# Windowed attention and a gated MLP in one kernel: the order of the MLP's products, of the weights' splits, and the places of late weight fetches

## The chip, the cores and the metric

The kernel runs on one core of one Trainium2 chip. The metric is device time in microseconds (us) of one execution. The core has a matrix engine (PE; its weight loads are shown as PEld), a vector engine (DVE), an activation engine (ACT), GpSimd (POOL) and a sync engine (SP) that issues most DMAs. The engines run side by side and wait for one another by semaphores; each takes its own instructions in order.

## What is computed

```
k_all, v_all = concat([k_g, k_l]), concat([v_g, v_l])          # 8 batches, 8 heads, 32 + 512 positions, 64 wide
out_g = softmax(q_g @ k_all.T / 8) @ v_all                      # 32 global queries see everything
s_l   = concat([q_l @ k_g.T / 8, where(|i - j| <= 32, q_l @ k_l.T / 8, -1e9)])
out_l = softmax(s_l) @ v_all                                    # local queries: a band and the globals
x = concat([out_g, out_l]) as 4352 rows of 512
h = x @ w_in                                                    # 512 x 2048
return (h * sigmoid(h)) @ w_out                                 # 2048 x 512
```

The inputs are float32, except w_in and w_out, which are float64.

## The kernel before, in words

The 4352 rows make 34 tiles of 128 rows, and the tiles make 12 token blocks n of SIZES = 3, ..., 3, 2, 2 tiles ("pieces"). Attention for a block is done ahead of that block's MLP. It comes as a stream of small steps with due times (`stream`); `advance` issues those that have come due, and `fill` does so in portions between the MLP's matmuls. For each of 128 steps k (a tile and a pair of heads) there are scores `s` on PE, a softmax on DVE and ACT (`probs`, `st`), a transposition and the product `o` with the values. From step 12 on the transposition goes by DMA: POOL copies `probs` into `halves`, SP stores them to DRAM (`away`, L379), and SP loads them back transposed into `pt` (L383). POOL adds the global part to `pt` (L401). `xh` and `xl` are the result in two parts, as below.

float32 products are made from pairs: every operand is a rounded upper part ("hi") and the rest ("lo"), and hi·hi + hi·lo + lo·hi stand for the product. So each product is three matmuls. The weights come as 16 slices f of 128 hidden units. A slice has two halves: w_in's 128x512 (half 0) and w_out's 128x512 (half 1). Each goes through three stages, all within block 0:
- `fetch_weights` (L193, SP): the raw float64 words come as a DMA into `raw_w`, 512 KB a half.
- `join_weights` (L209 on ACT, L211 and L212 on DVE): two 32-bit words become one float32.
- `split_weights` (L221 on ACT: `w_hi`; L222 on DVE: `w_lo`).

The tiles `ws0` to `ws15` hold the joined slice f at ws(f+1), later w_lo of slice f at ws(f). The tiles `wh0` to `wh15` hold first raw halves, later w_hi. Second halves of slices 8 to 15 have no such place: they come in two DMAs of 256 KB into pairs of the attention's tiles `qk` (odd slices) or `klo` (even).

The MLP goes through blocks n and in each through slices f. `first_layer(n, f)` makes twelve matmuls into one accumulator `h`; then tanh (`t`, L587 ACT and L588 DVE), `gh` (L590 ACT) and `gl` (L591 DVE). `second_layer(n, f)` comes one slice later, after the next `first_layer`: three matmuls for each piece into accumulators `out0` to `out2`, which add up over the 16 slices. At a block's end ACT copies them out (L612) and they are stored (L615).

PE's instructions stand in the order of the program text. The other engines' are put in an order by a scheduler when the program is built, except that those marked `hold` keep their mutual order. SP's DMAs stand in one queue.

Of the kernel before, what the change touches and what calls it, by code (L numbers as in the profile page):

```python
# [12 lines left out]
I32 = mybir.dt.int32  # L13
# [8 lines left out]
P = 128  # L22
# [5 lines left out]
SKV = SG + SL  # L28
DM, DFF = H * D, 2048
NCC, NF = DM // P, DFF // P  # L30
QW, KW, VW = 2 * P, 2 * W, 4 * D
# [7 lines left out]
SIZES = (3,) * 10 + (2, 2)  # L39
BUFS = dict(qk=2, raw=2, p=2, halves=1, pt=4)  # L40
# [7 lines left out]
SINGLE = 12  # L48
SCRATCH = 8
FETCH, LOOK = 5, 3  # L50
FIRSTW = {4: 2, 5: 2, 6: 1, 7: 1, 8: 1, 9: 1, 10: 1, 11: 1}
JOINS, SPLITS = (9.0, 9.6, 10.2, 10.8, 11.4, 12.0), (12.1, 12.7)

# [15 lines left out]
def attention_moe_kernel(ctx: ExitStack, tc: tile.TileContext, qk0_in, qk_in, v_in, gqk, wts, out):  # L69
    nc = tc.nc  # L70

    const = ctx.enter_context(tc.tile_pool(name="const", bufs=1))
    raws = ctx.enter_context(tc.tile_pool(name="raws", bufs=BUFS["raw"]))
    work = ctx.enter_context(tc.tile_pool(name="work", bufs=1))
# [33 lines left out]
    def scratch(i, dtype, name):  # L108
        return const.tile([P, 2 * DM], dtype, tag=f"wh{i}", name=name)
# [13 lines left out]
    for kind in range(3):  # L123
# [4 lines left out]
                                     fill=NEG, base=0, channel_multiplier=-1))  # L128
        hold(nc.gpsimd.affine_select(out=band, in_=band, pattern=[[-1, W - SG]], compare_op=ALU.is_ge,
                                     fill=NEG, base=2 * HALO, channel_multiplier=1))  # L130
# [49 lines left out]
    w_32, w_hi, w_lo, w_raw, w_next = [], [], [], {}, [0]  # L180

    def fetch_weights(f, half):
        i = 2 * f + half
        if half and f >= SCRATCH:
            tag, n = ("qk", QW + KW) if f % 2 else ("klo", SKV)
            homes_ = [work.tile([P, n], I32, tag=tag, bufs=BUFS["qk"], name=f"raw_w{i}_{q}")[:, :DM] for q in range(2)]
        else:
            taken.add(f + SCRATCH * half)
            homes_ = [scratch(f + SCRATCH * half, I32, f"raw_w{i}")]
        n = DM // len(homes_)  # L190
        w_raw[i] = [(raw, q * n, n) for q, raw in enumerate(homes_)]
        for raw, c0, n in w_raw[i]:
            hold(nc.sync.dma_start(out=raw, in_=wts[f, :, DM * half + c0 : DM * half + c0 + n].bitcast(I32)))  # L193

    def join_weights():
        i = w_next[0]
        w_next[0] += 1
        f = i // 2
        if f + 1 == NF:
            w_32.append(work.tile([P, SKV], F32, tag="klo", bufs=BUFS["qk"], name=f"w{i}")[:, :DM])  # L200
        elif i % 2 == 0:
            w = const.tile([P, 2 * DM], F32, tag=f"ws{f + 1}", name=f"w{f}")
            w_32.extend((w[:, :DM], w[:, DM:]))
        for raw, c0, n in w_raw[i]:
            join_words(w_32[i][:, c0 : c0 + n], raw)
# [9 lines left out]
    def split_weights(f):  # L215
        w_hi.append(const.tile([P, 2 * DM], F32R, tag=f"wh{f}", name=f"w_hi{f}"))
        w_lo.append(const.tile([P, 2 * DM], F32R, tag=f"ws{f}", name=f"w_lo{f}"))
        for c0 in range(0, 2 * DM, DM):
            sl = slice(c0, c0 + DM)
            hi, lo, w = w_hi[f][:, sl], w_lo[f][:, sl], w_32[2 * f + c0 // DM]  # L220
            hold(nc.scalar.copy(out=hi, in_=w))  # L221
            hold(nc.vector.tensor_tensor(out=lo, in0=w, in1=hi.bitcast(F32), op=ALU.subtract))  # L222
# [257 lines left out]
    def put(when, fn, *a):  # L480
        stream.append((when, fn, a))

    AHEAD = NPR
    for k, (t, b, c, pr) in enumerate(steps):
        a = (k, b, c, pr)
        j = k % NST
# [21 lines left out]
        if j == 0 and b:  # L508
            for hh in range(2):
                put(at + (TURN if b > 1 else TURN1)[hh], g_turn, b, hh)  # L510
        for i in range(FIRSTW.get(k, 0)):
            put(at + 0.01, fetch_weights, *divmod(sum(FIRSTW.get(j, 0) for j in range(k)) + i, 2))
        put(at + due["load"], st_load, *a)
# [10 lines left out]
        if k < SINGLE or pr == NPR - 1:  # L524
            n = 1 if k < SINGLE else NPR
# [17 lines left out]
    def advance(to):  # L543
        nonlocal done
        while done < len(stream) and stream[done][0] <= to:
            _, fn, a = stream[done]
            done += 1
            fn(*a)
# [7 lines left out]
    outs, now = {}, [0, 0]  # L556

    def fill(part):

        now[1] += part  # L560
        n = now[0]
        total = NF * SIZES[n] + (NF - 1) * SIZES[n] + (SIZES[n - 1] if n else 0)
        if n + 1 < len(SIZES):
            advance(ends[n] + (ends[n + 1] - ends[n]) * min(1.0, now[1] / total / FULL))

    def out_rows(t):
        kind, b, c = order[t]
        if kind == "l":
            return [(0, P, b * SKV + SG + c * P)]
        return [(SG * i, SG, (4 * b + i) * SKV) for i in range(4)]  # L570

    def first_layer(n, f):
        nt = SIZES[n] * P
        xh, xl = xblk[n]
        h = ps_h.tile([P, 512], F32, tag="h", name=f"h{n}_{f}")
        i = 0
        for c in range(NCC):
            wh = w_hi[f][:, c * P : (c + 1) * P]
            wl = w_lo[f][:, c * P : (c + 1) * P]
            for wt, x in ((wh, xh), (wh, xl), (wl, xh)):  # L580
                nc.tensor.matmul(h[:, :nt], wt, x[:, c, :nt], start=(i == 0), stop=(i == 3 * NCC - 1))  # L581
                i += 1
        t = two.tile([P, 3 * P], F32, tag="t", bufs=1, name=f"t{n}_{f}")
        gh = two.tile([P, 3 * P], F32R, tag="gh", name=f"gh{n}_{f}")
        gl = two.tile([P, 3 * P], F32R, tag="gl", name=f"gl{n}_{f}")

        nc.scalar.activation(t[:, :nt], h[:, :nt], AF.Tanh, scale=0.5)  # L587
        nc.vector.scalar_tensor_tensor(out=t[:, :nt], in0=t[:, :nt], scalar=1.0, in1=h[:, :nt], op0=ALU.add,  # L588
                                       op1=ALU.mult)
        nc.scalar.copy(out=gh[:, :nt], in_=t[:, :nt])  # L590
        nc.vector.tensor_tensor(out=gl[:, :nt], in0=t[:, :nt], in1=gh[:, :nt].bitcast(F32), op=ALU.subtract)  # L591
        return gh, gl

    def second_layer(n, f, gh, gl):
        if f == 0:
            outs[n] = [ps_out.tile([P, DM], F32, tag=f"out{i}", name=f"out{n}_{i}") for i in range(SIZES[n])]
        wh, wl = w_hi[f][:, DM:], w_lo[f][:, DM:]

        last = n + 1 == len(SIZES) and f == NF - 1
        for i in (reversed(range(SIZES[n])) if last else range(SIZES[n])):  # L600
            o = outs[n][i]
            sl = slice(i * P, (i + 1) * P)
            nc.tensor.matmul(o, gh[:, sl], wh, start=(f == 0), stop=False)  # L603
            nc.tensor.matmul(o, gh[:, sl], wl, start=False, stop=False)  # L604
            nc.tensor.matmul(o, gl[:, sl], wh, start=False, stop=(f == NF - 1))  # L605
            fill(1)
        if f == NF - 1:
            done_ = work.tile([P, 3 * DM], F32, tag=f"xh{n % 2}", name=f"o{n}")
            for i in (reversed(range(SIZES[n])) if last else range(SIZES[n])):
                o = outs[n][i]  # L610
                sb = done_[:, DM * i : DM * (i + 1)]
                nc.scalar.activation(sb, o, AF.Copy, scale=0.5)  # L612
                for p0, np_, r in out_rows(sum(SIZES[:n]) + i):
                    queue = nc.scalar if 0 < n < len(SIZES) - 1 else nc.sync
                    queue.dma_start(out=out[r : r + np_, :], in_=sb[p0 : p0 + np_, :])  # L615

    advance(ends[0])
# [2 lines left out]
    for n in range(len(SIZES)):  # L620
        for f in range(NF):
            if n == 0:
                while w_next[0] < 2 * min(NF, f + LOOK):
                    join_weights()
                for g, half in ((f + FETCH, 0), (f + FETCH - (f + FETCH > SCRATCH), 1)):
                    if g < NF and 2 * g + half not in w_raw:
                        fetch_weights(g, half)
            elif f == 0:
                advance(ends[n])
                now[:] = n, 0  # L630
            while len(w_hi) < NF and len(w_hi) <= NF * n + f + 1:
                split_weights(len(w_hi))
            g = first_layer(n, f)
            fill(SIZES[n])
            if pend is not None:
                second_layer(*pend)
            pend = (n, f, *g)
    second_layer(*pend)


# [67 lines left out]
```

## Time and profile before

| | |
|---|---|
| three runs | 986.2, 988.7 and 989.6 us; median 988.7 |
| profiled execution | 991.2 us, of it a span of 989.4 us from first to last instruction |
| busy, share of the span | PE 97%, PEld 86%, DVE 64%, ACT 58%, POOL 20% |
| granted PE clock | 0.993 of full speed over the span |
| matmuls | 5790, each with its own weight load |
| DMA | 157.3 MB, mean 159 GB/s |
| the three first-layer terms (L581) | 254.4, 254.0 and 252.8 us busy |
| the three second-layer terms (L603 to L605) | 220.9, 214.6 and 215.5 us busy |

Block 0's MLP begins at 48 us and ends at about 154 us. "Idle" and "waited" are time in which an engine's next instruction could not start, and the arrow names what ended it. Matmuls are pipelined, so that a matmul's own duration is longer than the distance from its start to the next one's; the distance is what it costs.

### The profile page before, as it was taken

What the parts mean: (1) busy time and instruction counts of PE and PEld (TensorE: products, weight loads), DVE (VectorE), ACT (ScalarE), POOL (GpSimd) and SP (SyncE); (2) the same over time, 40 slices, a digit from 0 to 9 for tenths busy, and PEclk for the clock granted to TensorE, in tenths of its full rate; (3) what the DMA queues carried; (4) which work ended last, traced back from release to release, by engine and by line L of the source; (5) the groups of instructions that cost most, each with busy time, mean ns of one, the idle gap of its engine ahead of it and who ended that gap; (6) DMA issues with size and microseconds to landing.
All of it is one profiled execution on the core that took longest, in us unless ns stands there. A gap on an engine that the chain in (4) does not pass through costs nothing.

```text
span 989.4 us, 17458 instructions
## 1 busy us (share of the span) xinstructions
PE 961.3 (97%) x5790; PEld 852.9 (86%) x5790; DVE 631.6 (64%) x1910; ACT 577.9 (58%) x1483; POOL 200.6 (20%) x413
## 2 busy tenths in 40 slices
PE   8989889999999999999999999999999999999997
PEld 6668778999898989998899999988989899889896
DVE  4888886766767667655577667766677565453322
ACT  7977756666556656644566666666566665343332
POOL 2112222122222212111222122212122221120000
PEclk9999899999999999999999999999999999999999
DMA  8699967566664666534656586565665564433000
GB/s 274 231 280 267 237 168 198 159 167 179 180 165 124 196 178 166 162 95 132 169 159 154 150 209 172 144 192 145 174 180 161 151 162 139 129 83 82 1 22 23
DMA packets 190026, 157.33 MB, mean 159 GB/s; under 512 B 128752, under 2 KB 148720, under 8 KB 189936
## 3 DMA queue, kind: packets, MB, share of 16 engines
q1 hardware_dynamic: 185712, 148.61, 55.1%
q10 hardware_dynamic: 4224, 7.60, 2.2%
q8 instruction: 46, 0.75, 0.3%
q14 instruction: 44, 0.36, 0.1%
HBM read 86.44 MB, written 39.32 MB: 127 GB/s over the span
## 4 chain that ended last, share of the span: by engine, by line
PE 79%; DVE 7%; DMA 6%; ACT 4%; issue 1%; SPq 1%; POOL 1%; DVEq 0%; ACTq 0%; POOLq 0%
PE h L581 33%; PE out L603 11%; PE out L605 11%; PE out L604 11%; PE o L425 6%; DMA raw<-in_qk_dram 3%; PE s L350 2%; PE s L351 2%; DMA raw_g<-in_gqk_dram 2%; DVE w L212 1%; DMA away<-halves 1%; DVE w_lo L222 1%; PE s L348 1%; ACT probs L359 1%; PE gt L296 1%
## 5 line engine op out<-in xcount | busy, mean ns | idle before, releaser
L581 PE MATMUL h<-xh,w_lo 128*128 128x384 f32 (+1 forms) x768 | 254.4, 331 | 8.8 <-DVE w_lo L222 8.8
L374 POOL COPY halves<-probs 128x512 uint16<-128x512 uint16 x232 | 153.0, 685 | 514.9 <-ACT probs L363 171.8
L581 PE MATMUL h<-xh,w_hi 128*128 128x384 f32 (+1 forms) x768 | 254.0, 331 | 0.4 <-ACT w_hi L221 0.4
L581 PE MATMUL h<-xl,w_hi 128*128 128x384 f32 (+1 forms) x768 | 252.8, 329 | 0.0
L603 PE MATMUL out<-w_hi,gh 128*128 128x512 f32 x544 | 220.9, 406 | 2.5 <-ACT gh L590 2.3
L605 PE MATMUL out<-w_hi,gl 128*128 128x512 f32 x544 | 215.5, 396 | 2.0 <-DVE gl L591 1.9
L604 PE MATMUL out<-w_lo,gh 128*128 128x512 f32 x544 | 214.6, 394 | 0.0
L587 ACT ACTIVATE t<-h 128x384 f32<-128x384 f32 (+1 forms) x192 | 90.4, 471 | 165.5 <-PE h L581 152.7
L588 DVE SCALAR_TENSOR_TENSOR t<-t,h 128x384 f32<-128x384 f32 (+1 forms) x192 | 101.7, 530 | 113.0 <-ACT t L587 112.4
L581 PEld LDWEIGHTS h<-xh,w_lo 128*128 128x128 f32 x768 | 145.6, 190 | 10.9 <-DVE w_lo L222 10.9
L359 ACT ACTIVATE probs<-probs,st 128x224 f32<-128x224 f32 x244 | 115.8, 476 | 65.0 <-DVE st L355 64.1
L581 PEld LDWEIGHTS h<-xh,w_hi 128*128 128x128 f32 x768 | 145.6, 190 | 8.0 <-ACT w_hi L221 0.9
L581 PEld LDWEIGHTS h<-xl,w_hi 128*128 128x128 f32 x768 | 145.5, 190 | 6.6 <-DVE xl L433 0.2
L591 DVE TENSOR_TENSOR gl<-t,gh 128x384 fp32r<-128x384 f32 (+1 forms) x192 | 109.4, 570 | 43.5 <-ACT gh L590 39.1
L355 DVE CUSTOM_DVE_ANT_0 probs<-s,mask 128x224 f32<-128x224 f32 x244 | 86.2, 388 | 78.9 <-PE s L351 66.7
L590 ACT CAST gh<-t 128x384 fp32r<-128x384 f32 (+1 forms) x192 | 94.4, 492 | 59.5 <-DVE t L588 59.2
L605 PEld LDWEIGHTS out<-w_hi,gl 128*128 128x128 f32 x544 | 102.5, 188 | 30.1 <-DVE gl L591 7.2
L603 PEld LDWEIGHTS out<-w_hi,gh 128*128 128x128 f32 x544 | 103.1, 190 | 22.0 <-ACT gh L590 6.1
L604 PEld LDWEIGHTS out<-w_lo,gh 128*128 128x128 f32 x544 | 103.2, 190 | 12.9
L332 ACT CAST qk<-raw 128x704 fp32r<-128x704 f32 x100 | 77.7, 777 | 25.8 <-DMA raw<-in_qk_dram 21.3
L363 ACT ACTIVATE probs<-probs,st 128x224 f32<-128x224 f32 x122 | 58.7, 481 | 43.4 <-DVE st L362 41.4
L333 DVE TENSOR_TENSOR klo<-raw,qk 128x448 fp32r<-128x448 f32 x100 | 64.5, 645 | 28.4 <-ACT qk L332 26.1
(91 smaller groups left out, 1075.8 us busy)
## 6 DMA issues: line engine op xcount, KB each, us to landing
raw<-in_qk_dram SPq DMA_DIRECT2D x100, 352.0 KB, 3.4
away<-halves SPq DMA_DIRECT2D x116, 256.0 KB, 2.8
vraw<-in_v_dram SPq DMA_DIRECT2D x30, 512.0 KB, 4.7
raw_w<-in_wts_dram SPq DMA_DIRECT2D x24, 512.0 KB, 6.6
raw_g<-in_gqk_dram SPq DMA_DIRECT2D x32, 304.0 KB, 4.2
out_dram<-o ACTq DMA_DIRECT2D x28, 256.0 KB, 3.3
raw<-in_qk_dram SPq DMA_DIRECT2D x28, 240.0 KB, 4.3
raw_w<-in_wts_dram SPq DMA_DIRECT2D x16, 256.0 KB, 3.7
```

What stands on the lines that cost most here:

```text
L332: nc.scalar.copy(out=qk, in_=raw)
L355: nc.vector.tensor_tensor_reduce(out=p[:, u, :W], in0=ss[u], in1=mask_of[c], scale=-SCALE, scalar=3.0e38, op0=ALU.add, op1=ALU.min, accum_ ...
L359: nc.scalar.activation(p[:, u, :W], p[:, u, :W], AF.Exp, bias=st[:, u : u + 1], scale=-1.0, accum_out=st[:, 2 + u : 3 + u])
L374: nc.gpsimd.tensor_copy(out=halves[:, :, u], in_=p[:, 2 * P * u : 2 * P * (u + 1)].bitcast(U16).rearrange("p (j h) -> p h j", h=2))
L581: nc.tensor.matmul(h[:, :nt], wt, x[:, c, :nt], start=(i == 0), stop=(i == 3 * NCC - 1))
L587: nc.scalar.activation(t[:, :nt], h[:, :nt], AF.Tanh, scale=0.5)
L588: nc.vector.scalar_tensor_tensor(out=t[:, :nt], in0=t[:, :nt], scalar=1.0, in1=h[:, :nt], op0=ALU.add, op1=ALU.mult)
L590: nc.scalar.copy(out=gh[:, :nt], in_=t[:, :nt])
L591: nc.vector.tensor_tensor(out=gl[:, :nt], in0=t[:, :nt], in1=gh[:, :nt].bitcast(F32), op=ALU.subtract)
L603: nc.tensor.matmul(o, gh[:, sl], wh, start=(f == 0), stop=False)
L604: nc.tensor.matmul(o, gh[:, sl], wl, start=False, stop=False)
L605: nc.tensor.matmul(o, gl[:, sl], wh, start=False, stop=(f == NF - 1))
```

## The change

First, the products are ordered by term. `first_layer` made the three terms for each of the four 128-row chunks c in turn. It now makes hi·hi for all chunks, then hi·lo, then lo·hi. `second_layer` made the three terms for each piece in turn. It now makes gh·w_hi for all pieces, then gh·w_lo, then gl·w_hi, except in a block's last slice, which keeps the order by piece.

Second, slice f + 1 is split at the head of slice f's round in block 0, ahead of the joins and the fetches of that round, and no longer behind them.

Third, the second halves of slices 8, 9, 10, 12 and 13 come in one DMA of 512 KB into `ws15`, `ws14`, `ws13`, `ws14` and `ws15`, the places of later lower weights; those of slices 11 and 14 into `klo` and that of 15 into `qk`, in two pieces as before.

Fourth, ACT issues the very last output DMA, and SP the other four of the last block.

```diff
+PLACES = ("ws15", "ws14", "ws13", "klo", "ws14", "ws15", "klo", "qk")
...
         if half and f >= SCRATCH:
-            tag, n = ("qk", QW + KW) if f % 2 else ("klo", SKV)
-            homes_ = [work.tile([P, n], I32, tag=tag, bufs=BUFS["qk"], name=f"raw_w{i}_{q}")[:, :DM] for q in range(2)]
+            tag = PLACES[f - SCRATCH]
+            if tag in ("qk", "klo"):
+                n = QW + KW if tag == "qk" else SKV
+                homes_ = [work.tile([P, n], I32, tag=tag, bufs=BUFS["qk"], name=f"raw_w{i}_{q}")[:, :DM] for q in range(2)]
+            else:
+                homes_ = [const.tile([P, 2 * DM], I32, tag=tag, name=f"raw_w{i}")]
...
-        for c in range(NCC):
-            wh = w_hi[f][:, c * P : (c + 1) * P]
-            wl = w_lo[f][:, c * P : (c + 1) * P]
-            for wt, x in ((wh, xh), (wh, xl), (wl, xh)):
-                nc.tensor.matmul(h[:, :nt], wt, x[:, c, :nt], start=(i == 0), stop=(i == 3 * NCC - 1))
+        for wt, x in ((w_hi[f], xh), (w_hi[f], xl), (w_lo[f], xh)):
+            for c in range(NCC):
+                nc.tensor.matmul(h[:, :nt], wt[:, c * P : (c + 1) * P], x[:, c, :nt], start=(i == 0),
+                                 stop=(i == 3 * NCC - 1))
                 i += 1
...
-        for i in (reversed(range(SIZES[n])) if last else range(SIZES[n])):
-            o = outs[n][i]
-            sl = slice(i * P, (i + 1) * P)
-            nc.tensor.matmul(o, gh[:, sl], wh, start=(f == 0), stop=False)
-            nc.tensor.matmul(o, gh[:, sl], wl, start=False, stop=False)
-            nc.tensor.matmul(o, gl[:, sl], wh, start=False, stop=(f == NF - 1))
-            fill(1)
+        terms = ((gh, wh), (gh, wl), (gl, wh))
+        if f < NF - 1:
+            order_ = [(i, j) for j in range(3) for i in range(SIZES[n])]
+        else:
+            order_ = [(i, j) for i in (reversed(range(SIZES[n])) if last else range(SIZES[n])) for j in range(3)]
+        for done_, (i, j) in enumerate(order_, 1):
+            g, w = terms[j]
+            nc.tensor.matmul(outs[n][i], g[:, i * P : (i + 1) * P], w, start=(f == 0 and j == 0),
+                             stop=(f == NF - 1 and j == 2))
+            if done_ % 3 == 0:
+                fill(1)
...
-                    queue = nc.scalar if 0 < n < len(SIZES) - 1 else nc.sync
+                    queue = nc.sync if n == 0 or last and i else nc.scalar
...
             if n == 0:
+                split_weights(f + 1) if 0 < f < NF - 1 else None
                 while w_next[0] < 2 * min(NF, f + LOOK):
                     join_weights()
...
-            while len(w_hi) < NF and len(w_hi) <= NF * n + f + 1:
-                split_weights(len(w_hi))
```

The names in the following rows carry the block and the slice (h0_4 is block 0, slice 4), and a number of the buffer behind. Lines of the changed kernel are 3 to 8 higher than before.

On PE, at block 0's slice 4, before: the end of the first layer of slice 4, the scores of step 16, and the second layer of slice 3.

```order
L581 MATMUL h0_4_979<-xh_0_244,w_hi4_912 128x384
L581 MATMUL h0_4_979<-xl_0_245,w_hi4_912 128x384
L581 MATMUL h0_4_979<-xh_0_244,w_lo4_913 128x384
L348 MATMUL s16_1002<-raw16_873 128x224 x2
L603 MATMUL out0_0_804<-w_hi3_843,gh0_3_932 128x512
L604 MATMUL out0_0_804<-w_lo3_844,gh0_3_932 128x512
L605 MATMUL out0_0_804<-w_hi3_843,gl0_3_933 128x512
L603 MATMUL out0_1_805<-w_hi3_843,gh0_3_932 128x512
L604 MATMUL out0_1_805<-w_lo3_844,gh0_3_932 128x512
L605 MATMUL out0_1_805<-w_hi3_843,gl0_3_933 128x512
```

And now, the whole first layer of slice 4 and what follows:

```order
L584 MATMUL h0_4_977<-xh_0_244,w_hi4_899 128x384 x4
L584 MATMUL h0_4_977<-xl_0_245,w_hi4_899 128x384 x4
L584 MATMUL h0_4_977<-xh_0_244,w_lo4_900 128x384 x4
L353 MATMUL s16_1000<-raw16_873 128x224 x2
L611 MATMUL out0_0_804<-w_hi3_832,gh0_3_930 128x512
L611 MATMUL out0_1_805<-w_hi3_832,gh0_3_930 128x512
L611 MATMUL out0_2_806<-w_hi3_832,gh0_3_930 128x512
L611 MATMUL out0_0_804<-w_lo3_833,gh0_3_930 128x512
L611 MATMUL out0_1_805<-w_lo3_833,gh0_3_930 128x512
L611 MATMUL out0_2_806<-w_lo3_833,gh0_3_930 128x512
L611 MATMUL out0_0_804<-w_hi3_832,gl0_3_931 128x512
```

The first matmul that needs w_lo is now the ninth of twelve, and the first that needs gl the seventh of nine; an accumulator is written in turn with the two others.

On the DVE, at the same place before: the joins of slice 5 (raw_w10, raw_w11 into w5), then the lower weights of slice 4.

```order
L281 TENSOR_SCALAR pg1_128<-pg1_128,gst1_1_890 128x544
L211 TENSOR_SCALAR raw_w10_725<-raw_w10_725 128x512
L212 SCALAR_TENSOR_TENSOR w5_899<-w5_899,raw_w10_725 128x512
L211 TENSOR_SCALAR raw_w11_727<-raw_w11_727 128x512
L212 SCALAR_TENSOR_TENSOR w5_899<-w5_899,raw_w11_727 128x512
L222 TENSOR_TENSOR w_lo4_913<-w4_832,w_hi4_912 128x512 x2
L361 TENSOR_SCALAR st15_943<-st15_943 128x2
L591 TENSOR_TENSOR gl0_3_933<-t0_3_931,gh0_3_932 128x384
```

And now:

```order
L286 TENSOR_SCALAR pg1_128<-pg1_128,gst1_1_890 128x544
L227 TENSOR_TENSOR w_lo4_900<-w4_838,w_hi4_899 128x512 x2
L216 TENSOR_SCALAR raw_w10_725<-raw_w10_725 128x512
L217 SCALAR_TENSOR_TENSOR w5_905<-w5_905,raw_w10_725 128x512
L216 TENSOR_SCALAR raw_w11_727<-raw_w11_727 128x512
L366 TENSOR_SCALAR st15_941<-st15_941 128x2
L592 SCALAR_TENSOR_TENSOR t0_4_990<-t0_4_990,h0_4_977 128x384
```

The split stands ahead of the joins; the second half of the join comes some rows later, behind slice 4's tanh product and the next softmax.

On SP, around the second halves of slices 8 and 9 (raw_w17 and raw_w19), before:

```order
L193 DMA raw_w17_0_908<-in_wts_dram 128x512
L193 DMA raw_w17_1_909<-in_wts_dram 128x512
L383 DMA_TRANSPOSE pt2_131<-away14_897 128x4x256
L310 DMA raw17_956<-in_qk0_dram 128x480
L193 DMA raw_w18_971<-in_wts_dram 128x1024
L379 DMA away15_1014<-halves15_999 128x1024
L310 DMA raw18_1024<-in_qk0_dram 128x480
L193 DMA raw_w20_1036<-in_wts_dram 128x1024
L193 DMA raw_w19_0_1038<-in_wts_dram 128x512
L193 DMA raw_w19_1_1039<-in_wts_dram 128x512
L383 DMA_TRANSPOSE pt3_132<-away15_1014 128x4x256
```

And now:

```order
L198 DMA raw_w17_914<-in_wts_dram 128x1024
L388 DMA_TRANSPOSE pt2_131<-away14_897 128x4x256
L315 DMA raw17_954<-in_qk0_dram 128x480
L198 DMA raw_w18_975<-in_wts_dram 128x1024
L384 DMA away15_1012<-halves15_997 128x1024
L315 DMA raw18_1022<-in_qk0_dram 128x480
L198 DMA raw_w20_1040<-in_wts_dram 128x1024
L198 DMA raw_w19_1042<-in_wts_dram 128x1024
L388 DMA_TRANSPOSE pt3_132<-away15_1012 128x4x256
```

The order of the queue is the same; a pair of fetches has become one.

## The prediction

> **What bounds the kernel now.** I read the stretches of the run first, then who waits for whom in each, then single instructions. In the windows the columns after the bounds are the length, then PE, PEld, DVE, ACT and POOL busy, the granted clock, the DMA engines' share and GB/s. The first row is token block 0 from its third weight slice up to its last (slices 2 to 14); the second lies within it; the third is everything after block 0.
>
> ```profile
> 56.90:145.00 88.10, 77.06 (x396) 65.93 (x396) 76.65 (x213) 60.40 (x157) 19.29 (x30) 0.94 0.89 240
> 75.00:100.00 25.00, 23.95 (x144) 21.13 (x144) 22.43 (x64) 18.07 (x48) 6.55 (x10) 1.00 0.93 268
> 152.30:989.40 837.10, 825.32 (x5002) 742.17 (x5000) 512.00 (x1523) 466.99 (x1178) 167.15 (x331) 1.00 0.53 144
> ```
>
> After block 0, PE is busy 825.3 of 837.1 us and DVE 61%: TensorE bounds, and only its own waits can be won. In block 0 PE and DVE are both at 87% (77.1 and 76.7 of 88.1 us), at a clock of 0.94. Who waits there:
>
> ```profile
> PEld h L581 <- DVE w_lo L222: 10.9, 7, 2.9
> PE h L581 <- DVE w_lo L222: 8.8, 5, 2.6
> DVE w L212 <- ACT w L209: 2.6, 6, 0.5
> PE o L425 <- POOL pt L401: 1.0, 1, 1.0
> ```
>
> Nearly all of PE's waiting in block 0 is for the lower weights w_lo that the DVE makes (us in total, times, longest). One such wait, PE and then DVE:
>
> ```profile
> 68.82 0.34 PE L581 MATMUL h<-xh,w_hi 128*128 128x384 f32 x1
> 68.99 0.34 PE L581 MATMUL h<-xl,w_hi 128*128 128x384 f32 x1
> 71.95 0.69 PE L581 MATMUL h<-xh,w_lo 128*128 128x384 f32 x1 [2.62 <-DVE w_lo L222]
> 72.44 0.52 PE L581 MATMUL h<-xh,w_hi 128*128 128x384 f32 x1
> 72.76 0.52 PE L581 MATMUL h<-xl,w_hi 128*128 128x384 f32 x1
> 68.94 0.42 DVE L211 TENSOR_SCALAR raw_w<-raw_w 128x512 uint32<-128x512 uint32 x1
> 69.47 0.69 DVE L212 SCALAR_TENSOR_TENSOR w<-w,raw_w 128x512 uint32<-128x512 uint32 x1
> 70.08 0.42 DVE L211 TENSOR_SCALAR raw_w<-raw_w 128x512 uint32<-128x512 uint32 x1
> 70.61 0.69 DVE L212 SCALAR_TENSOR_TENSOR w<-w,raw_w 128x512 uint32<-128x512 uint32 x1
> 71.21 1.28 DVE L222 TENSOR_TENSOR w_lo<-w,w_hi 128x512 fp32r<-128x512 f32 x2
> ```
>
> The third matmul of slice 4 needs w_lo. The DVE joins the halves of a later slice from 68.94 to 71.21 (2.27 us) before it splits this one. PE stands still until 71.95, and then runs at half pace: starts 0.32 us apart (72.44 to 72.76) where 0.17 is usual (68.82 to 68.99). The same follows a second such wait, of 2.14 us at 106.3; its second-layer matmuls were 0.42 us apart (first two rows), where full pace is 0.22 to 0.23 (last four):
>
> ```profile
> 110.13 0.63 PE L604 MATMUL out<-w_lo,gh 128*128 128x512 f32 x1
> 110.55 0.63 PE L605 MATMUL out<-w_hi,gl 128*128 128x512 f32 x1
> 649.96 0.39 PE L605 MATMUL out<-w_hi,gl 128*128 128x512 f32 x1
> 650.18 0.39 PE L603 MATMUL out<-w_hi,gh 128*128 128x512 f32 x1
> 650.41 0.39 PE L604 MATMUL out<-w_lo,gh 128*128 128x512 f32 x1
> 650.64 0.39 PE L605 MATMUL out<-w_hi,gl 128*128 128x512 f32 x1
> ```
>
> Eighteen first-layer matmuls at about 0.15 us too much and six of the second layer at 0.2 make 3.9 us lost to the lower clock. The Trainium skill (TensorE: Matmul & The Clock Gate, "Why this matters for your kernels") names idle gaps above some 3 us as what drops the clock. The trace shows drops around waits of 2.6 and 2.1 us, so the measurement decides; by that rule the 3.9 us would not hang on these waits, PE's floor below would stay at 77.1, and the floor rival would end at 973.6 instead of 971.2.
>
> **The first layer's order and the earlier split.** All twelve matmuls stay, and so do their weight loads. w_lo is wanted after eight matmuls instead of two: 6 x 0.17 = 1.0 us later. The split stands ahead of the next join, so w_lo comes up to 2.27 us sooner. The 3.3 us together exceed the longest wait (2.9), so taken singly every wait goes: about 11 us, plus 3.9 us of clock. But the joins do not vanish; they move behind the split, and what follows them on the DVE (tanh products, softmax) is late by what w_lo gained. So block 0's floor is a sum of work:
> - PE: 77.06 - 3.9 = 73.2 us.
> - DVE: 76.65 us, less what the larger places save. Five second halves (slices 8, 9, 10, 12 and 13) are now joined whole, not in two pieces (groups of 48 to 152 us):
>
> ```profile
> L212 DVE SCALAR_TENSOR_TENSOR w<-w,raw_w 128x512 uint32<-128x512 uint32 x18 | 13.5, 747 | 3.5 <-ACT w L209 2.6
> L211 DVE TENSOR_SCALAR raw_w<-raw_w 128x512 uint32<-128x512 uint32 x18 | 7.6, 421 | 0.0
> L212 DVE SCALAR_TENSOR_TENSOR w<-w,raw_w 128x256 uint32<-128x256 uint32 x16 | 7.1, 446 | 0.8
> L211 DVE TENSOR_SCALAR raw_w<-raw_w 128x256 uint32<-128x256 uint32 x16 | 5.4, 340 | 0.0
> ```
>
> Two pieces take 2 x (446 + 340) = 1572 ns, one 747 + 421 = 1168: 0.40 us each, 2.0 us for five. So the DVE floor is 74.65 us, and the DVE becomes the slower of the two. How near it gets: from 75 to 100 us, with no long PE wait, it was busy 22.43 of 25 us, 90%. The waits of its L212 for ACT (2.6 of 88.1 us, 3%) should go: the DVE now has the split (1.28 us) to do before its part of a join, while ACT, a step ahead in the same order, does its own. At 93% the stretch takes 74.65/0.93 = 80.3 us: 7.8 us gained. Ends: 90% gives 82.9 (5.2 gained), 96% gives 77.8 (10.3).
>
> **The places.** In the old places a fetch waits until the join two slices earlier is done, and everything behind it on SP stands too:
>
> ```profile
> 83.72 6.04 SPq L193 DMA_DIRECT2D raw_w<-in_wts_dram  x3
> SPq L193 <- DVE raw_w L211: 14.3, 4, 4.9
> ```
>
> Behind this one stand a transpose, an away store and attention loads. The five new fetches find their place unused or joined at least an iteration before, and SP issues five DMAs fewer of the same bytes. PE waited only 1.0 us for attention there, so I cost this at nothing by itself. It is the cover for the faster block: with the same transfers the DMA share of 0.89 rises to 0.89 x 88.1/80.3 = 0.98, and transposed probabilities or raw loads are what is late next.
>
> **The second layer's order.** gl is wanted after six matmuls, not two: 4 x 0.23 = 0.92 us later (not in a block's last slice, which keeps its order). Waits after block 0, and one of them:
>
> ```profile
> PEld out L605 <- DVE gl L591: 6.5, 12, 1.3
> PE out L605 <- DVE gl L591: 1.9, 4, 0.8
> PEld out L603 <- ACT gh L590: 5.6, 13, 1.5
> 653.25 0.50 PE L603 MATMUL out<-w_hi,gh 128*128 128x512 f32 x1
> 653.60 0.39 PE L604 MATMUL out<-w_lo,gh 128*128 128x512 f32 x1
> 654.29 0.50 PE L605 MATMUL out<-w_hi,gl 128*128 128x512 f32 x1 [0.31 <-DVE gl L591]
> 654.63 0.40 PE L603 MATMUL out<-w_hi,gh 128*128 128x512 f32 x1
> ```
>
> Here gl cost (0.69 - 0.23) + (0.34 - 0.23) = 0.57 us. Over all, the loss lies between PE's own idle 1.9 and the weight loads' 6.5; I take 4.0, as part of the loads' wait hides under the matmul before. The waits for gh stay: gh is still the first thing wanted. Against it: a new block's accumulator for its third piece is written at the third matmul, not the seventh. At this block start the copy that frees it ends at 653.70:
>
> ```profile
> 653.10 0.60 ACT L612 ACTIVATE o<-out 128x512 f32<-128x512 f32 x1
> ```
>
> The third matmul would start at about 653.25 + 0.35 + 0.23 = 653.83, only just after. I take off 0.7 us for this over eleven block starts (ends 0 and 2). Net 3.3.
>
> **The last output.** SP issued five DMAs at the end; now four, and ACT the fifth, right behind its last copy:
>
> ```profile
> 983.28 1.29 ACT L612 ACTIVATE o<-out 128x512 f32<-128x512 f32 x2 [1.05 <-PE out L605]
> 983.91 2.22 SPq L615 DMA_DIRECT2D out_dram<-o  x5
> DMA to landing us min/median/max: 1.7/1.7/2.1
> ```
>
> The fifth goes out at 983.28 + 1.29 = 984.6 instead of 983.91 + 2.22 - 0.43 = 985.7. SP's fourth, issued at 985.2, then lands last, some 0.5 to 0.9 us sooner. I take 0.8 (ends 0 and 1).
>
> **Sum.** 7.8 + 3.3 + 0.8 = 11.9 us. The profiled execution took 991.2 us (span 989.4): it would take 979.3. The median of the three runs is 988.7, 2.5 below that execution, so I forecast 988.7 - 11.9 = 976.8, said as 977. Own range, without all ends at once: 973 to 983 (5.2 + 0.5 + 0 to 10.3 + 4.5 + 0.9).
>
> **Rivals.**
> - Waits move on. The DVE is the pace of block 0 already, and a PE released from w_lo waits for gl, softmax or transposes instead. For it: the DVE's 87% and the join work that only changed place. Against: its idle eighth, part of it behind a standing PE. At 87% the stretch takes 74.65/0.87 = 85.8: 2.3 gained; with 4.1 from the rest, 982.3.
> - Block 0 reaches the DVE floor: 88.1 - 74.65 = 13.4, with 4.1, gives 971.2. Against: a DMA share that would be over 1.0 there.
> - Nothing measurable: block 0 gains 2.3 and gl's waits come back as waits for gh, 986.
> - Slower: the second layer now writes out0, out1, out2 in turn. It changes accumulator at every matmul, not every third: 6 more times a slice in ten three-piece blocks and 4 in two, over 15 slices, is 900 + 120 = 1020. If a change costs, it decides from (11.9 + 3)/1020 = 15 ns on. The rows at 649.96 to 650.64 speak against it: 0.22 us over a change, 0.23 without. If each change started like the 0.35 of 653.25 to 653.60, it would be 1020 x 0.12 = 122 us, 1099. More mildly, if each of the eleven later blocks lost 3.9 us to the clock as block 0 did, 977 + 43 = 1020. The Trainium skill (TensorE: Matmul & The Clock Gate, "A second HAM failure mode: psum-queue depth-cycling") tells of such a kernel: cycling through banks left small idle gaps, and the clock kept dropping. This trace has a clock of 1.00 after 152 us with a change every third matmul, so it bears that out only weakly.
>
> **How the numbers follow.** Forecast 0.58, waits move on 0.19, DVE floor 0.12, nothing 0.07, slower 0.04. Under 0.3% (3 us) a measurement of this kernel can hardly tell from no change. So faster 0.58 + 0.19 + 0.12 = 0.89, same 0.07, slower 0.04. The range runs from the floor case to just short of the no-change case: 970.5 to 986.
>
> **What would show it.** Right: the wait of h for w_lo under 2 us in all, a clock of 1.00 throughout, block 0's stretch near 80 us with DVE over 90%, no SP stand of 5 us at a weight fetch, gl's waits under 2 us, gh's still near 5. Wrong: a DVE share still at 87% with new waits of L605 or o, starts of the second layer over 0.24 us apart, or o's copies as a new releaser at block starts.

## The result, and the profile after

| | before | after |
|---|---|---|
| median of the runs | 988.9 us (4 runs, 986.2 to 989.6) | 977.7 us (4 runs, 976.3 to 981.2) |
| profiled execution | 991.2 us, span 989.4 | 977.4 us, span 975.5 |
| mean granted clock | 0.993 | 0.998 |

By the medians it is 11.2 us faster, where 11.9 were forecast. The ratio of the means is 0.9897, with an interval of 0.9865 to 0.9929, which is 10.2 us. The same kernel in two more comparisons gave 0.9892 and 0.9907 (below).

The windows of the changed kernel (length; PE, PEld, DVE, ACT, POOL busy; clock; DMA share; GB/s), for the first and the last of the stretches shown of before:

```profile
57.10:135.40 78.30, 72.00 (x397) 62.35 (x396) 73.87 (x200) 59.57 (x149) 20.18 (x30) 1.00 0.95 266
...
142.60:975.50 832.90, 823.65 (x5002) 743.58 (x5000) 511.00 (x1523) 467.12 (x1178) 170.74 (x331) 1.00 0.54 145
```

These rows and those of before account for the 13.9 us between the two spans. That is 2.7 us more than between the medians: the profiled execution of before took 991.2 us, longer than any of its four runs. Block 0's stretch went from 88.10 to 78.30, 9.8 us. Everything from block 1 on went from 837.1 to 832.9, 4.2 us. What is left, before the stretch and between the two, is 0.1 us longer together. In the stretch PE is busy 72.0 us and the DVE 73.9 of 78.3: the DVE at 94% is now the slower of the two, and the clock is 1.00.

Who waited in that stretch (us in total, times, longest): rows of PE (its matmuls) and PEld (its weight loads), in their order.

```profile
PEld h L584 <- ACT w_hi L226: 5.9, 5, 2.5
...
PE h L584 <- ACT w_hi L226: 3.7, 4, 2.0
...
PEld s L353 <- DMA raw<-in_qk_dram: 2.0, 2, 1.2
PEld o L430 <- POOL pt L406: 1.4, 1, 1.4
```

No row has h waiting for w_lo, where there were 10.9 us. Nor does the DVE's join wait for ACT any more (2.6). In their place stands a wait for the upper weights w_hi, which ACT makes: 5.9 us of the weight loads, 3.7 of PE's matmuls (before, for w_lo: 10.9 and 8.8). Slice 4, PE and then DVE, shows how the first layer now runs through:

```profile
68.57 0.87 PE L584 MATMUL h<-xh,w_hi 128*128 128x384 f32 x4
69.28 0.86 PE L584 MATMUL h<-xl,w_hi 128*128 128x384 f32 x4
69.99 0.86 PE L584 MATMUL h<-xh,w_lo 128*128 128x384 f32 x4
...
69.06 1.28 DVE L227 TENSOR_TENSOR w_lo<-w,w_hi 128x512 fp32r<-128x512 f32 x2
70.26 0.42 DVE L216 TENSOR_SCALAR raw_w<-raw_w 128x512 uint32<-128x512 uint32 x1
```

The row of the DVE holds both halves of slice 4's w_lo; the first, which the first layer uses, is done after some 0.69 us (what a single one takes), at about 69.75, and the four matmuls that need it start at 69.99 without a wait. The join comes behind, at 70.26. Slice 14 shows the new wait, PE and then ACT:

```profile
130.34 0.96 PE L584 MATMUL h<-xh,w_hi 128*128 128x384 f32 x4 [2.04 <-ACT w_hi L226]
...
128.89 0.51 ACT L594 CAST gh<-t 128x384 fp32r<-128x384 f32 x1
129.31 0.48 ACT L368 ACTIVATE probs<-probs,st 128x224 f32<-128x224 f32 x1
129.69 1.12 ACT L226 CAST w_hi<-w 128x512 fp32r<-128x512 f32 x2
```

The cast that makes w_hi comes behind the cast of gh and the scaling of a head's probabilities on ACT, and PE, which now asks for nothing else, stands 2.04 us for it. ACT in turn had stood for the DVE just before, 0.75 us until 126.92 and 0.36 us until 127.78.

From block 1 on, the second layer waits for its two halves of the activation:

```profile
PEld out L611 <- ACT gh L594: 6.9, 13, 2.2
...
PEld out L611 <- DVE gl L595: 1.2, 3, 0.7
```

gl went from 6.5 to 1.2 us. gh's went from 5.6 to 6.9, and in the two other executions of the changed kernel that were profiled it is 8.4 and 8.5.

### The profile page after: what moved, and what is told of

Same layout as the page of the kernel before. It is cut to its first block, busy times and chain, and to the rows that moved or that the text cites. A ratio compares the mean times of both kernels' runs of the same rounds, so it can differ in the third digit from the quotient of the medians.

```text
span 975.5 us, 17432 instructions
## 1 busy us (share of the span) xinstructions
PE 954.1 (98%) x5790; PEld 850.3 (87%) x5790; DVE 629.4 (65%) x1900; ACT 578.2 (59%) x1478; POOL 204.1 (21%) x413
## 4 chain that ended last, share of the span: by engine, by line
PE 86%; DVE 6%; DMA 4%; ACT 2%; issue 1%; SPq 0%; ACTq 0%; DVEq 0%
PE h L584 35%; PE out L611 35%; PE o L430 6%; DMA raw<-in_qk_dram 3%; PE s L355 2%; PE s L356 2%; PE s L353 1%; DVE w L217 1%; DVE w_lo L227 1%; DMA pt<-away 1%; DVE raw_w L216 1%; PE gt L301 1%; DMA away<-halves 1%; DVE probs L360 1%; PE t L397 1%
## 5 line engine op out<-in xcount | busy, mean ns | idle before, releaser
L611 PE MATMUL out<-w_hi,gh 128*128 128x512 f32 x544 | 164.8, 401 | 3.7 <-ACT gh L594 3.6
L584 PE MATMUL h<-xh,w_hi 128*128 128x384 f32 (+1 forms) x768 | 160.9, 331 | 3.8 <-ACT w_hi L226 3.7
L611 PE MATMUL out<-w_hi,gl 128*128 128x512 f32 x544 | 161.9, 396 | 0.2 <-DVE gl L595 0.2
L611 PE MATMUL out<-w_lo,gh 128*128 128x512 f32 x544 | 161.3, 394 | 0.0
L584 PE MATMUL h<-xl,w_hi 128*128 128x384 f32 (+1 forms) x768 | 158.7, 328 | 0.3 <-DVE xl L438 0.3
L584 PE MATMUL h<-xh,w_lo 128*128 128x384 f32 (+1 forms) x768 | 158.0, 327 | 0.0
L584 PEld LDWEIGHTS h<-xh,w_hi 128*128 128x128 f32 x768 | 133.4, 189 | 19.5 <-ACT w_hi L226 5.9
L584 PEld LDWEIGHTS h<-xl,w_hi 128*128 128x128 f32 x768 | 133.1, 189 | 0.6 <-DVE xl L438 0.6
L584 PEld LDWEIGHTS h<-xh,w_lo 128*128 128x128 f32 x768 | 131.4, 188 | 0.0
L611 PEld LDWEIGHTS out<-w_lo,gh 128*128 128x128 f32 x544 | 100.5, 188 | 21.6 <-issue 0.6
L611 PEld LDWEIGHTS out<-w_hi,gh 128*128 128x128 f32 x544 | 93.5, 189 | 16.2 <-ACT gh L594 6.9
```

Of the source, the lines that this page charges most:

```text
L584: nc.tensor.matmul(h[:, :nt], wt[:, c * P : (c + 1) * P], x[:, c, :nt], start=(i == 0), stop=(i == 3 * NCC - 1))
L611: nc.tensor.matmul(outs[n][i], g[:, i * P : (i + 1) * P], w, start=(f == 0 and j == 0), stop=(f == NF - 1 and j == 2))
```

## The experiments

Twelve programs ran, two of them the changed kernel again, in four comparisons, each with the kernel before on the same chip. The medians of before were 991.7, 990.0, 991.7 and 990.9 us, so ratios are compared and not times. The times in the first four expectations count from 988.7 us, so a measured ratio times 988.7 is what to hold against them.

### The four parts by themselves

The first layer's order alone, in the kernel before:

```diff
-        for c in range(NCC):
...
-            for wt, x in ((wh, xh), (wh, xl), (wl, xh)):
...
+        for wt, x in ((w_hi[f], xh), (w_hi[f], xl), (w_lo[f], xh)):
+            for c in range(NCC):
...
```

> Before, with the first layer's order by term alone. By the theory of the prediction (w_lo comes late, the order buys 1.0 us for each of seven waits): waits of h for w_lo fall from 10.9 to about 5 us, the clock still drops once, 983 to 986 us. By the rival that only the DVE's work sets block 0's length: nothing is saved, 987 to 990 us.

Measured: 988.5 us, ratio 0.9966 (0.9945 to 0.9988), or 985.3 of 988.7. Its waits in block 0, in a profile of the longest of its twelve runs (995.4 us):

```profile
PEld h L579 <- DVE w_lo L222: 7.2, 7, 1.5
...
PEld h L579 <- ACT w_hi L221: 2.5, 3, 1.9
```

The wait for w_lo fell from 10.9 to 7.2 us, not to the 5 expected, and its longest from 2.9 to 1.5. The gain is 3.4 us by the ratio, inside what the theory of the prediction had expected.

The split ahead of the joins alone, in the kernel before:

```diff
+                split_weights(f + 1) if 0 < f < NF - 1 else None
                 while w_next[0] < 2 * min(NF, f + LOOK):
...
-            while len(w_hi) < NF and len(w_hi) <= NF * n + f + 1:
-                split_weights(len(w_hi))
```

> Before, with the split ahead of the next joins alone. By the theory of the prediction: w_lo comes up to 2.27 us sooner, its waits fall to 1 to 2 us, no drop of the clock, 981 to 984 us. By the rival that only the DVE's work counts: 987 to 990 us.

Measured: 994.4 us, ratio 1.0029 (1.0008 to 1.005): slower, which neither the theory nor the rival had expected. Its waits in block 0, of PE and then of SP's queue, and one of SP's:

```profile
PE s L348 <- DMA raw<-in_qk_dram: 8.9, 5, 3.6
...
PEld h L581 <- DVE w_lo L222: 1.5, 3, 0.7
...
SPq L193 <- DVE w L212: 24.6, 11, 8.1
...
80.53 9.64 SPq L193 DMA_DIRECT2D raw_w<-in_wts_dram  x3
```

The split did what it was to do: w_lo's wait is 1.5 us. But the joins stand behind it, and in the old places a fetch waits on SP for a join. SP stood 24.6 us at weight fetches (before: 14.3 and 8.9), once 9.64 us in a row, and the raw loads of the attention that queue behind it on SP came late: PE waited 8.9 us for them (before: 0.4). This profile is of the kernel's shortest execution (990.1 us), which is no slower than before's; it shows the exchange of waits, while the loss is that of twelve runs and was not seen in a profile.

The second layer's order alone:

```diff
+        terms = ((gh, wh), (gh, wl), (gl, wh))
...
+            order_ = [(i, j) for j in range(3) for i in range(SIZES[n])]
...
```

> Before, with the second layer's order by term alone. By the theory of the prediction: waits for gl after block 0 fall from 6.5 to under 2 us, those for gh stay, 984.5 to 987 us, and second-layer starts stay 0.23 us apart. By the rival that a change of accumulator at every matmul costs: starts over 0.24 us apart and no gain, 989 us or more.

Measured: 989.1 us, ratio 0.9969 (0.995 to 0.9988), or 985.6 of 988.7: a gain of 3.1 us by the ratio, as the theory expected. After block 0 the wait for gl is 1.2 us here too, and gh's 7.2.

The larger places alone:

```diff
+            tag = PLACES[f - SCRATCH]
...
+                homes_ = [const.tile([P, 2 * DM], I32, tag=tag, name=f"raw_w{i}")]
```

> Before, with the new places of late second halves alone. By the theory of the prediction: SP's long stands at weight fetches go and 2.0 us of DVE work, 986 to 989 us. By the rival that SP's stands were what held block 0 up: 981 to 985 us.

Measured: 989.3 us, ratio 0.9978 (0.9956 to 1.0), a gain of 2.2 us that the interval does not keep apart from none. SP's long stands at weight fetches are gone, w_lo's wait is not (10.9 before): the top row of SP's waits in block 0, and PE's for w_lo.

```profile
SPq L388 <- DMA away<-halves: 23.5, 9, 4.3
...
PEld h L586 <- DVE w_lo L227: 10.0, 8, 2.7
```

### The split with the places

The kernel before with the two edits of the split and the places together:

> Before, with the split ahead and the new places together, both orders of products as before. By the theory that the split alone was slow since the later joins kept SP standing at the old places: raw loads make PE wait under 3 us in block 0 (8.9 with the split alone), waits for w_lo stay at 1 to 2 us, ratio to before 0.990 to 0.995. By the rival that the earlier split itself holds up attention on the DVE: waits for raw loads or softmax stay, ratio 0.998 or more.

Measured: 985.6 us, ratio 0.9946 (0.9924 to 0.9968). In block 0:

```profile
PEld h L586 <- DVE w_lo L227: 3.5, 8, 1.0
...
PE s L353 <- DMA raw<-in_qk_dram: 1.8, 2, 1.6
...
SPq L198 <- DVE w L217: 5.3, 3, 2.8
```

With the places, SP's stand at the fetches falls from 24.6 to 5.3 us and PE's wait for raw loads from 8.9 to 1.8; the wait for w_lo is 3.5 us, more than the 1 to 2 expected. The split that costs 0.29% by itself now comes with a gain of 0.54%, against 0.22% for the places alone. The places are what makes it harmless.

### The split taken out of the whole

The changed kernel with the split behind the joins and fetches, as before:

```diff
-                split_weights(f + 1) if 0 < f < NF - 1 else None
...
+            while len(w_hi) < NF and len(w_hi) <= NF * n + f + 1:
+                split_weights(len(w_hi))
```

> The changed kernel, with the split behind the joins and fetches of its round as before. By the theory of the prediction (the order of the first layer buys 1.0 us, the earlier split the rest): waits of h for w_lo of 4 to 8 us in block 0, slices 2 to 14 in 81 to 85 us, ratio to before 0.992 to 0.996. By the rival that with order and places alone the DVE already sets the pace: under 2 us of such waits, within 1.5 us of the changed kernel's 0.989 to 0.991.

Measured: 981.8 us, ratio 0.9896 (0.9871 to 0.9922), where the changed kernel had 0.9897, 0.9892 and 0.9907 on other chips. The window of block 0's stretch, and its waits:

```profile
57.16:137.89 80.73, 73.30 (x396) 61.83 (x395) 73.55 (x201) 59.34 (x151) 18.94 (x30) 1.00 0.96 261
...
PEld h L584 <- DVE w_lo L227: 6.3, 7, 1.3
...
PEld h L584 <- ACT w_hi L226: 3.3, 6, 1.9
```

w_lo's wait is back (6.3 us), as the theory expected, and w_hi's is smaller (3.3 instead of 5.9); no single wait of PE is longer than 1.9 us. The time is what the rival expected: no loss shows, though intervals of some 0.3% leave room for one of up to 3 us. The stretch takes 80.7 us, a little longer than the 76.6 to 80.3 of the three executions with the split, with the same 73.6 us of DVE work. So with the order by term the split ahead mainly changes which operand PE waits for; that it brings nothing at all is not shown.

### The second layer's order taken out of the whole

```diff
-        terms = ((gh, wh), (gh, wl), (gl, wh))
...
+        for i in (reversed(range(SIZES[n])) if last else range(SIZES[n])):
...
+            nc.tensor.matmul(o, gh[:, sl], wh, start=(f == 0), stop=False)
+            nc.tensor.matmul(o, gh[:, sl], wl, start=False, stop=False)
+            nc.tensor.matmul(o, gl[:, sl], wh, start=False, stop=(f == NF - 1))
+            fill(1)
```

> The changed kernel, with the second layer's order by piece as before. By the theory of the prediction: waits for gl after block 0 are back at 5 to 7 us, 2 to 4 us slower than the changed kernel. By the rival that a wait for gl removed comes back as a wait for gh: within 1 us of the changed kernel.

Measured: 984.4 us, ratio 0.9927 (0.9905 to 0.9949); the changed kernel in the same comparison 982.0. After block 0:

```profile
PEld out L607 <- ACT gh L594: 7.4, 14, 1.7
PEld out L609 <- DVE gl L595: 6.5, 12, 1.3
```

gl's wait is back to its 6.5 us, and it costs 2.4 us by the medians. Alone it had brought 3.1. The two intervals allow more and less, but the size is near the prediction's 3.3. gh's wait is 7.4 us here, between the 6.9 and 8.5 of the changed kernel's executions, so this pair shows no exchange of gl's wait for gh's; against before's 5.6 a part of it is not ruled out.

### Is the DVE the pace of block 0?

Each join's two operations on the DVE replaced by one, which leaves out the three lowest bits of the weights' mantissas:

```diff
-        hold(nc.vector.tensor_scalar(out=low, in0=low, scalar1=29, scalar2=None, op0=ALU.logical_shift_right))
-        hold(nc.vector.scalar_tensor_tensor(out=wi, in0=wi, scalar=3, in1=low, op0=ALU.logical_shift_left,
-                                            op1=ALU.bitwise_or))
+        hold(nc.vector.tensor_scalar(out=wi, in0=wi, scalar1=3, scalar2=None, op0=ALU.logical_shift_left))
```

> The changed kernel, with less DVE work in the joins: the shift of the low words is left out, and the second operation has no second input (the weights lose their three lowest mantissa bits). By the theory that the DVE sets block 0's pace: slices 2 to 14 take 73 to 75 us instead of 78.3, at PE's own 72, and the kernel is 3 to 5 us faster than the changed one. By the rival that DMA (share 0.95) or the waits between the engines set it: 77 us or more, and no more than 1 us faster.

Measured: 975.0 us, ratio 0.9844 (0.9812 to 0.9877); the changed kernel beside it 980.2. The stretch, and PE's first wait in it:

```profile
55.88:130.60 74.72, 70.99 (x396) 62.76 (x395) 59.15 (x176) 60.84 (x153) 16.21 (x30) 1.00 1.01 283
...
PEld s L351 <- DMA raw<-in_qk_dram: 3.3, 3, 1.4
```

With the DVE at 59.2 us instead of some 73.5, the first layer waits for neither w_hi nor w_lo, and the run is 5.3 us shorter by the medians. In the profiles the stretch is 1.9 to 5.6 us shorter than in the three executions of the changed kernel, and PE, at 71.0 of 74.7 us, is now the busier engine. The DMA share went up to 1.01, so the transfers had not been the limit at 0.95. So the DVE's work set the stretch. What is late next are the raw loads.

Then the other way: in the slices from 2 on, the half of w_lo that the second layer uses is subtracted on POOL.

```diff
-            hold(nc.vector.tensor_tensor(out=lo, in0=w, in1=hi.bitcast(F32), op=ALU.subtract))
+            sub = (nc.gpsimd if c0 and f > 1 else nc.vector).tensor_tensor
+            hold(sub(out=lo, in0=w, in1=hi.bitcast(F32), op=ALU.subtract))
```

> The changed kernel, with the lower weights of the second halves of slices 2 to 15 made by POOL instead of the DVE (14 subtractions of 0.64 us each off the DVE, nothing left out). By the theory that the DVE sets block 0's pace: slices 2 to 14 take 1 to 3 us less than the 76.6 to 78.3 of the changed kernel, and the kernel is 1 to 3 us faster. By the rival that POOL is slow at it and holds up halves and the DVE: the second layer waits for w_lo, 0 to 5 us slower than the changed kernel.

Measured: 986.6 us, ratio 0.9948 (0.9931 to 0.9966); the changed kernel beside it 982.0, so 4.6 us slower, where the theory had expected 1 to 3 us less. The stretch, PE's longest wait in it, and the joins' groups (us in all, mean ns) with those of the changed kernel behind:

```profile
57.25:140.45 83.20, 73.72 (x396) 61.75 (x395) 77.20 (x188) 58.15 (x147) 34.79 (x40) 1.00 0.90 252
...
PE out L612 <- ACT gh L595: 6.2, 3, 3.5
...
L217 DVE SCALAR_TENSOR_TENSOR w<-w,raw_w 128x512 uint32<-128x512 uint32 x23 | 21.3, 924 | 1.0
L216 DVE TENSOR_SCALAR raw_w<-raw_w 128x512 uint32<-128x512 uint32 x23 | 20.7, 901 | 0.0
```

```profile
L217 DVE SCALAR_TENSOR_TENSOR w<-w,raw_w 128x512 uint32<-128x512 uint32 x23 | 16.2, 706 | 1.0
L216 DVE TENSOR_SCALAR raw_w<-raw_w 128x512 uint32<-128x512 uint32 x23 | 11.3, 493 | 0.0
```

The DVE was rid of fourteen of its subtractions: they fell from 21.6 us (29 of them) to 10.4 (15). But the joins grew by (21.3 - 16.2) + (20.7 - 11.3) = 14.5 us. Its busy time in the stretch rose from 73.9 to 77.2, 3.3 us, and the stretch became longer too. The rival had the size right (0 to 5 us slower) and the path wrong: the second layer hardly waited for w_lo (0.4 us), but 6.2 us for gh. At the longest of these waits, ACT had stood 2.36 us until 99.05 for the softmax on the DVE, which stood behind shifts of 1.52 and 0.83 us. More DVE time made the kernel slower and less made it faster: both runs say that the DVE is the pace. Neither keeps the sum of its work apart from the lateness of single steps, since both change with the joins.

### The changed kernel again, and its loss in block 1

> The changed kernel once more, as the measure for the others on this chip: ratio to before 0.987 to 0.993.

Measured: 980.2 us, ratio 0.9892 (0.9857 to 0.9928). The stretch took 76.6 us with the DVE at 96%:

```profile
56.16:132.74 76.58, 71.80 (x397) 62.26 (x395) 73.29 (x200) 59.26 (x149) 19.31 (x30) 1.00 0.95 270
```

> The changed kernel, as the measure for the others on this chip: ratio to before 0.987 to 0.993.

Measured: 982.0 us, ratio 0.9907 (0.9873 to 0.9941). Here one clock drop shows as 0.98:

```profile
57.18:137.45 80.27, 73.91 (x397) 63.70 (x395) 75.19 (x203) 60.65 (x153) 19.58 (x30) 0.98 0.97 265
```

The first profiled execution lost some 2 us in block 1: a raw load came late, ACT's cast of it, then gh, then PE. In SP's queue ahead of that load stood block 0's store of its output.

```profile
160.38 0.78 ACT L337 CAST qk<-raw 128x704 fp32r<-128x704 f32 x1 [1.94 <-DMA raw<-in_qk_dram]
...
161.62 0.96 PE L611 MATMUL out<-w_hi,gh 128*128 128x512 f32 x3 [2.00 <-ACT gh L594]
...
SPq L623 <- ACT o L620: 4.1, 1, 4.1
```

To see whether that store is the cause, ACT issued it instead:

```diff
-                    queue = nc.sync if n == 0 or last and i else nc.scalar
+                    queue = nc.sync if last and i else nc.scalar
```

> The changed kernel, with the output stores of block 0 issued by ACT instead of SP. By the theory that the store at 146 us held SP up for 4.1 us and so made a raw load, ACT's copy of it and gh late: the 2.0 us wait for gh at 161 us and the clock's drop there go, 2 to 3 us less than the changed kernel in the same call. By the rival that this wait comes from elsewhere: no difference over 1 us.

Measured: 978.7 us, ratio 0.9879 (0.9843 to 0.9915), 1.6 us less than the changed kernel beside it, between what the theory and the rival expected, with intervals that overlap. Its profile has no wait for gh there. The two other executions of the changed kernel have one, of 1.60 us until 158.59 and 2.12 us until 163.81, each behind a raw load that ACT waited 2.09 and 2.04 us for, and neither lost any clock there. That three executions with the store on SP have the wait and one without has not speaks for the store; how a store at 146 us makes a load 10 us later late is not shown, and the cause stays open.

## Why the prediction was right, point by point

- **The sum** came nearer than its terms. By the medians it missed by 0.7 us, by the ratio by 1.7. Of the 10.2 us by the ratio, 3.1 are the second layer's by itself and 1.2 the last output's, which leaves 5.9 for block 0, where 7.8 were forecast; the pair of profiles gives 9.8, with a slow execution of before. Intervals of 0.3% do not decide between these. So the way the prediction bounded block 0 is borne out, and that the sum came so near is in part luck.
- **Block 0's stretch** (80.3 forecast; 78.3, 76.6 and 80.3 in three executions). The bound held: DVE work of 74.65 us was forecast and 73.9, 73.3 and 75.2 were measured. The share was 94, 96 and 94% where I took 93. PE's 73.2 came out as 72.0: the two half-speed windows of before (71.6 to 75.0 and 105.7 to 112.5) hold 9.2 us of PE's work, so they cost some 4.6 us and not the 3.9 that I counted from single matmuls.
- **"Taken singly every wait goes"** failed. w_lo's wait went to nothing, but 5.9 us of w_hi's came up. I had priced the moved split by what PE waits for and not by what PE would ask for next. The sum did not suffer, since it rested on the work of the DVE, which is the same whichever operand is late.
- **The split ahead**: of the 3.3 us of lead I gave 2.27 to the split and 1.0 to the order. Alone, the order brought 0.34% and the split lost 0.29%; in the whole no gain of the split shows. The order, places, second layer and tail without the split give 0.34 + 0.22 + 0.31 + 0.12 = 0.99% (the tail from its 1.2 us, below), and that kernel measured 1.04%, the whole 1.03%.
- **The places at nothing, but for 2.0 us of joins**: alone 0.22%, 2.2 us by the ratio (0 to 4.4), near the 2.0 us that the saved joins were to be worth, if it is not nothing. That they are also the cover for the moved split, 0.29% slower without them and 0.54% faster with them, I had not seen; I called them the cover for the faster block's transfers.
- **SP**: no stand of 5 us at a weight fetch, as forecast. Of SP's waits in the stretch the longest at a fetch was 2.1 us:

```profile
SPq L198 <- DVE w L217: 3.2, 3, 2.1
```

- **DMA share and what is late next**: 0.98 forecast, 0.95 measured; raw loads and transposed probabilities were named, and their waits are 2.0 and 1.4 us.
- **The second layer**: 4.0 us for gl less 0.7. Measured 3.1 alone and 2.4 in the whole. The copies that free an accumulator, where I took off 0.7, hold up weight loads for 0.4 us in all. At the start of block 7, of which the prediction spoke, PE first waits 0.42 us for gh, and then the third piece's weight load 0.20 us for ACT's copy (L620):

```profile
643.52 1.00 PE L611 MATMUL out<-w_hi,gh 128*128 128x512 f32 x3 [0.42 <-ACT gh L594]
...
644.02 0.19 PEld L611 LDWEIGHTS out<-w_hi,gh 128*128 128x128 f32 x1 [0.20 <-ACT o L620]
```

  gl's 6.5 and 1.9 us bracket both measurements. That the 4.0 was too large, since more of the weight loads' wait had been hidden than I took, fits but is not shown. gh's wait, which was to stay near 5, is 6.9 to 8.5.
- **The last output**: 0.8 forecast. From PE's last matmul to the end of the span it is 975.5 - 971.2 = 4.3 us, and was 5.5 (983.9 to 989.4).

```profile
971.20 1.75 SPq L623 DMA_DIRECT2D out_dram<-o  x4
971.90 0.34 ACTq L623 DMA_DIRECT2D out_dram<-o  x1
```

  ACT's DMA goes out at 971.9 beside SP's four, which take until 972.95: about 1.2 us gained, a little over the 0.8.
- **Accumulators in turn** cost nothing. Later in block 7, three matmuls in turn take 0.69 us from their start to the next three's, 0.23 each as before, and the last window has a clock of 1.00:

```profile
654.19 0.85 PE L611 MATMUL out<-w_lo,gh 128*128 128x512 f32 x3
654.88 0.86 PE L611 MATMUL out<-w_hi,gl 128*128 128x512 f32 x3
```

  The Trainium skill (TensorE: Matmul & The Clock Gate, "A second HAM failure mode: psum-queue depth-cycling") tells of a kernel whose clock kept dropping under such cycling; this one does not show it.
- **"A clock of 1.00 throughout"** failed. The first profiled execution kept it in block 0 and lost it once, behind the wait of 2.00 us at 161.6: the window from 162.9 to 166.3.

```profile
162.90:166.30 3.40, 3.40 (x11) 2.83 (x10) 2.91 (x7) 1.39 (x3) 0.94 (x2) 0.50 0.98 190
```

  All 3.4 us of PE there are at half speed, so it costs 1.7 us. That is a drop behind a 2.0 us gap, which bears out the prediction's choice of the measurement over the 3 us that the Trainium skill (TensorE: Matmul & The Clock Gate, "Why this matters for your kernels") names. The third execution lost as much inside block 0, and the second nothing. More on the clock stands at the end.
- **Rivals**: waits did move on, from w_lo to w_hi, but the DVE's share did not stay at 87%. The floor of 74.65 was neared and not reached (76.6 at the least). The rivals that forecast no measurable gain and a slower kernel did not come.

## What to carry to other kernels

Where two engines share a stretch, sum the work of each first: here the DVE's sum told the length of block 0, whichever operand came late. Two changes that take away the same wait do not add up: the order by term and the earlier split both aimed at w_lo, and beside the order no gain of the split shows. What is then left is had by less work on the engine that sets the pace. A product whose operands come at different times should use the latest one last, which cost nothing here and asked nothing of another engine. A step that is moved ahead delays the steps behind it: before it is credited, follow what they free, down to the queue that waits for it and what is queued there.

## What the runs showed of the hardware

POOL's work can hold the DVE up. In the run with the lower weights on POOL, the DVE's shift took 1.53 us where it takes 0.42 by itself (slice 4 above, at 70.26):

```profile
102.35 1.30 POOL L228 TENSOR_TENSOR w_lo<-w,w_hi 128x512 fp32r<-128x512 f32 x1 [3.98 <-ACT w_hi L226]
...
101.80 0.69 DVE L228 TENSOR_TENSOR w_lo<-w,w_hi 128x512 fp32r<-128x512 f32 x1 [0.47 <-ACT w_hi L226]
102.41 1.53 DVE L216 TENSOR_SCALAR raw_w<-raw_w 128x512 uint32<-128x512 uint32 x1
```

It starts 0.06 us after POOL's subtraction and ends 0.3 us after it: it waited for nearly all of it. The Trainium skill (SBUF — State Buffer, "Who interferes with whom") says that the two engines share one pair of ports, that the instruction that comes second is blocked until the first is done, and that it holds for some forms only; the rows agree. The subtraction itself took 1.30 us on POOL and 0.69 on the DVE.

The clock does not drop at a fixed length of wait. The wait for w_hi at slice 14 was 2.04 us in the first profiled execution and 2.07 in the third. In the first the clock stayed (window around the wait, first row); in the third it was halved from 132.4, 1.6 us after the wait ended at 130.84 (second row, the stretch from there). The four drops looked at so far, two of before and two of the changed kernel, come behind waits of 2.0 to 2.6 us and last 3.4 us, one of them 6.8. Over all the runs not even that holds: with the lower weights on POOL, a wait of 3.48 us that ended at 100.54 left the clock at 1.00 (window 99 to 104), and without the second layer's order the matmuls ran at half pace from about 479.2, behind a wait of 1.40 us that ended at 477.42. Thirteen of the fourteen profiled executions have at least one such stretch before PE's last matmul.

```profile
128.00:136.00 8.00, 5.96 (x31) 5.27 (x30) 7.73 (x24) 6.64 (x18) 2.67 (x4) 1.00 0.40 109
```

```profile
132.40:135.80 3.40, 3.40 (x11) 3.14 (x10) 3.06 (x10) 2.00 (x5) 1.15 (x2) 0.50 0.46 137
```

Runs of the same program came out about 1% apart (before: 987.9 to 997.1 us in the first comparison), so that parts worth 0.3% needed twelve runs each and stand here with intervals that nearly reach 1, or do.
